# Another written order for the first batch of a fused attention and low-rank mixer kernel

## The chip, the cores and the metric

The kernel runs on one core of a Trainium2 chip. The metric is the device time of one execution in microseconds (us), as the median of several runs. Engines are named as in the profile: PE is TensorE, ACT ScalarE, DVE VectorE, POOL GpSimd, SP the queue that issues most DMAs.

## The reference

Attention with normalised queries and keys, then a mixer and an MLP over its output, for 8 batches, 12 heads, 448 tokens and a head size of 64 (768 = 12 x 64 columns):

```python
q_n, k_n = rmsnorm(q, g_q), rmsnorm(k, g_k)          # x / sqrt(mean(x*x) + 1e-6) * g, over the 64
scores = (q_n @ k_n.T) / sqrt(64)
attn = exp(scores - max); attn = attn / sum(attn)
x = (attn @ v) laid out as [batch, 448, 768]
h = x.transpose(0, 2, 1) @ U @ V                      # mixes the 448 tokens, rank 32
u = x + h.transpose(0, 2, 1)
out = u + relu(u @ w_ch1) @ w_ch2                     # 768 -> 3072 -> 768
```

All inputs and the output are float32; the products run in bf16.

## The kernel before

Heads go in **groups** of four (three groups a batch, numbered through: group 0 to 2 are batch 0), and the attention works on **pairs** of heads, six a batch. Of each group, q and k are loaded by SP, squared (`sq`, line 141 on ScalarE, line 144 on GpSimd), summed over the 64 on VectorE (`sm`, line 167), and turned into roots on ScalarE as a logarithm and an exponential (`rt`, lines 944 and 950 or 953). The rows are then scaled (`sc`, line 957), transposed on TensorE into a PSUM tile (`turn`, line 368) and copied out: q on ScalarE or VectorE with the product of both gains (`tq`, lines 375 and 377), k on VectorE (`tk`, lines 383 and 386). Group 0 is cut in two parts along the tokens (`sqp`, `smp`, `rt0`, `scp`, with the part as their last number: part 0 is 512 elements a partition wide, part 1 is 384), so that its first steps can run on two engines at once.

A pair has four score steps (`S.pair.row`, line 430): rows 0 to 2 are 128 keys for both heads of the pair, row 3 the last 64 keys of both. Each score step writes one of two PSUM tiles of its pool, and an exponential on ScalarE (`E.pair.row`, line 435) empties it; so S.5.1 has to wait for E.4.3. Rows 0 to 2 are 128x896 exponentials, row 3 is 128x448. Then come the products with v (`V.pair.half`, lines 500 and 504) on TensorE and the division by the sum (`N.pair.half`, lines 513 and 514) on VectorE. `val` casts the values of a group on GpSimd (lines 206 and 208), and the loads of the group three further on are issued behind it.

For batch 0 the mixer is done in chunks of columns: `mt` (line 648) multiplies the tokens by U, `mtc` (line 652) copies the result, `mix` (lines 657 to 660) multiplies by V and adds x, `mc` (lines 664 and 666) copies the mixed, transposed columns into `uT`, and `u` (line 711) are the first products with `w_ch1`, for 4 of its 24 slices of 128 columns. `prepu` and `prepv` (lines 342, 343, 333 and 335, GpSimd) lay U and V out for this, and `ms` (`fill_mixer`) fills the buffers with zeros and ones beforehand, among them the margins of a key buffer. `b.n` are n matmuls of 128x128 on the identity (line 245), whose result nobody reads: they only keep TensorE running. Their tile comes from the same pool of four PSUM banks as the transposes and the products. `w` issues a load of a part of `w_ch1` from GpSimd's queue, in the order of the list `todo` (768, 1152, 1152 and 1536 KB); `gr`, `gains`, `pg` and `gg` prepare the product of the gains.

All of batch 0 up to there is a list of steps written out by hand, the string `FRONT`. A step is a name, its numbers, and after a colon its engine (a, v, p for ScalarE, VectorE, GpSimd). The program is recorded in this order, and each engine runs its own instructions in the order of recording, waiting for what they need:

```python
for step in FRONT.split():
    step, _, eng = step.partition(":")
    name, *a = step.split(".")
    steps[name](*map(int, a), engines[eng])
    if name == "val":
        load(int(a[0]) + 3)
```

Behind `FRONT` a planner goes through the attention of the other batches (`att`) and the MLP (`mlp`, from `up`, line 693, on) by costs and due times; it starts from fixed values there, so that what `FRONT` does doesn't change its order. The up-products use slices of `w_ch1` as they come (`up`, line 693), the down-products `w_ch2` (`down`, line 740).

Of the kernel before, what the change touches and what calls it, by code (L numbers as in the profile page):

```python
# [27 lines left out]
def kernel(  # L28
# [13 lines left out]
    nc = tc.nc  # L42
    B, H, S, D = q.shape
# [209 lines left out]
    def fill_values(i, eng):  # L253
        va, vl = va_bufs[i], vl_bufs[i]
        eng.memset(va[:, :, D:D1], 1.0)
        eng.memset(vl, 0.0)
        for e in range(2):
            eng.memset(vl[e * R:(e + 1) * R, :, e * D1 + D:(e + 1) * D1], 1.0)

    def fill_keys(i, eng):  # L260
        eng.memset(kT_bufs[i][D:P, :, SM:S], 0.0)
        eng.memset(kT_bufs[i][0:D, :, S:], 0.0)

    for i in range(2):
        fill_values(i, nc.vector)
    fill_keys(0, nc.vector)
    for e in range(2):
        nc.gpsimd.tensor_mul(gp[:, e * D:(e + 1) * D], grow[:, 0, :], grow[:, 1, :])

    gg = consts.tile([P, 2], FP32)  # L270
# [74 lines left out]
    def fill_mixer():  # L345
        nc.gpsimd.memset(Uz, 0.0)
        fill_values(2, nc.gpsimd)
        fill_keys(1, nc.gpsimd)


    at = {"pe": 0.0, "act": 0.0, "dve": 0.0}
# [429 lines left out]
    for i, (b, pr) in enumerate(pairs):  # L781
        if b == 0:
            continue
        gi, a = divmod(i, 2)
# [85 lines left out]
    for b in range(B):  # L870
# [24 lines left out]
    mlp.extend((3.9 * w, down_end, (B - 1, cols[-1], piece), B - 1) for piece, w in enumerate((1.0, 0.67, 0.34)))  # L895

    FRONT = """
        sqp.0.1:a sqp.0.0:p gr smp.0.1 sqp.1.1:a sqp.1.0:p smp.0.0 rt0.0.1 smp.1.1 gains:p smp.1.0 rt0.1.1 pg rt0.0.0 b.22
        scp.0.1:v scp.1.1:p rt0.1.0 scp.0.0:v sq.1.0:a scp.1.0:p gg turn.0.0 sm.1.0 ms tq.0.0:a turn.0.1 b.17 w tk.0.0 rt.1.0
        sq.1.1:a tq.0.1:v S.0.1 sc.1.0:v S.0.0 b.13 sq.2.0:p E.0.0 sm.1.1 turn.1.0 E.0.1 S.0.2 val.0 tk.0.1 E.0.2 tq.1.0:v b.5  # L900
        sm.2.0 S.0.3 b.8 E.0.3 S.1.0 rt.1.1 tq.1.1:v sq.2.1:p S.1.1 V.0.1 E.1.0 sc.1.1:v b.7 E.1.1 S.1.2 turn.1.1 sm.2.1 E.1.2
        S.1.3 V.0.0 tk.1.0 val.1 E.1.3 N.0.1 rt.2 tk.1.1 sc.2.0:p sc.2.1:v S.2.0 V.1.0 E.2.0 S.2.1 prepu N.1.0 E.2.1 S.2.2
        N.0.0 V.1.1 w E.2.2 turn.2.1 N.1.1 prepv S.2.3 b.4 tk.2.0 E.2.3 S.3.0 E.3.0 tk.2.1 S.3.1 w turn.2.0 V.2.0 E.3.1 tq.2.1:v
        S.3.2 N.2.0 mt.0 E.3.2 tq.2.0:v S.3.3 V.2.1 val.2 mtc.0 E.3.3 S.4.0 N.2.1 E.4.0 S.4.1 V.3.1 w V.3.0 E.4.1 N.3.1 S.4.2
        mix.1 N.3.0 E.4.2 S.4.3 sq.3.0:p mt.1 mc.1:v E.4.3 S.5.0 mtc.1 E.5.0 S.5.1 V.4.0 sq.3.1:p V.4.1 E.5.1 N.4.0 S.5.2 mix.0
        N.4.1 E.5.2 S.5.3 mix.2 mc.0:v mix.3 E.5.3 sm.3.0 u.0.0 mc.2:a u.1.0 mt.2 mc.3:a u.0.1 u.1.1 mtc.2 V.5.0 sm.3.1 u.2.0
        u.2.1 V.5.1 N.5.0 rt.3 u.3.0 u.3.1 N.5.1 u.0.3 u.1.3 u.2.3 u.3.3 mt.3 u.0.2 mix.4 mtc.3 u.1.2 mix.5 mc.4:a u.2.2 u.3.2
        mc.5:a u.0.4 u.1.4 u.2.4 u.3.4 u.0.5 u.1.5 u.2.5 u.3.5
    """
    engines = {"a": nc.scalar, "v": nc.vector, "p": pool, "": None}  # L910
    beside = uT.rearrange("p k c -> p (k c)")[:, :4 * NT * D].bitcast(FP32).rearrange("p (j d) -> p j d", d=D)
# [43 lines left out]
    def scale_by(gi, i, eng, lo=0, hi=NT):  # L955
# [8 lines left out]
        "smp": lambda i, p, eng: sums_part(i, *PARTS[p]),  # L964
        "rt0": lambda i, p, eng: (log_part(i, p), root_part(i, p)),
        "ms": lambda eng: fill_mixer(),
        "scp": lambda i, p, eng: scale_by(0, i, eng, *PARTS[p]),
        "gr": lambda eng: most_gain(),
# [82 lines left out]
    while ia < len(att) or im < len(mlp):  # L1051
# [10 lines left out]
        if take_att:  # L1062
            c, f, a = att[ia]
# [13 lines left out]
        else:  # L1077
# [6 lines left out]
            c, f, a, _ = mlp[im]  # L1084
# [35 lines left out]
```

## Time and profile before

| | us |
|---|---|
| median of 3 runs | 572.04 |
| lowest and highest | 571.39, 573.68 |
| the profiled execution, its own time | 570.46 |
| its span in the profile | 568.7 |
| TensorE busy in the span | 561.5 |
| ScalarE busy in the span | 308.5 |

The granted clock of TensorE is 0.999 of full speed in the profiled execution. In the lines of the profile a time in front of a row is its start in us from the span's start, then its length; `x4` behind it counts instructions that were merged into one row. Brackets show how long the engine was idle before it, and what ended that. Rows of one engine may overlap a little, as an instruction begins before the one ahead has quite ended.

### The profile page before, as it was taken

The numbers are of one execution on the slowest core, as the hardware profiler recorded it, in microseconds if no ns is written. First come the engines' busy times: TensorE is split into PE (matmuls) and PEld (weight loads), VectorE is DVE, ScalarE is ACT, GpSimd is POOL, SyncE is SP. The second block draws the span as 40 slices with busy tenths as digits, with TensorE's granted clock in tenths as the row PEclk, the third lists the DMA queues.
The fourth block names the chain that finished last, engine by engine and source line by source line (L and its number), as shares of the span: only waits on it lengthen the run. The fifth ranks groups of instructions, "written<-read, shape, count | busy, mean of one in ns | idle before, by whom it ended". The sixth has DMA issues, their size and how long they took to land.

```text
span 568.7 us, 11567 instructions
## 1 busy us (share of the span) xinstructions
PE 561.5 (99%) x4756; PEld 321.9 (57%) x4756; DVE 189.4 (33%) x425; ACT 308.5 (54%) x518; POOL 204.5 (36%) x308
## 2 busy tenths in 40 slices
PE   8899999999999999999999999999999999999997
PEld 7665555555555555555556555565465555555555
DVE  6955564312443222521235231532034210410011
ACT  6967760888454776287553677367752544014300
POOL 6874784355332724343522532351531000000000
PEclk9999999999999999999999999999999999999999
DMA  9999999784247633595335735375215200320022
GB/s 241 223 242 240 247 228 179 159 225 114 62 91 171 170 98 63 90 233 144 74 96 107 203 90 125 67 204 128 36 33 86 56 23 0 77 56 0 1 57 56
DMA packets 104830, 68.20 MB, mean 120 GB/s; under 512 B 66633, under 2 KB 100937, under 8 KB 104777
## 3 DMA queue, kind: packets, MB, share of 16 engines
q1 hardware_dynamic: 95124, 57.83, 44.2%
q0 software_dynamic: 9408, 9.44, 10.0%
q8 instruction: 37, 0.61, 0.5%
q10 hardware_dynamic: 244, 0.20, 0.1%
q14 instruction: 17, 0.13, 0.1%
HBM read 52.20 MB, written 11.01 MB: 111 GB/s over the span
## 4 chain that ended last, share of the span: by engine, by line
PE 94%; ACT 4%; DMA 1%; DVE 0%; POOL 0%; issue 0%; POOLq 0%
PE po L740 38%; PE ph L693 37%; PE pv L541 4%; ACT E L435 3%; PE sc L464 2%; PE sl L455 2%; PE sl L476 2%; PE pr L568 1%; PE po L727 1%; PE pv L537 1%; PE sc L430 1%; PE sc L711 1%; PE sc L626 1%; PE pu L609 1%; DMA ob<-in_g_k_dram 1%; PE pt L368 1%
## 5 line engine op out<-in xcount | busy, mean ns | idle before, releaser
L693 PE MATMUL ph<-uT,w1b 128*128 128x448 bf16 x1128 | 223.9, 352 | 0.0
L740 PE MATMUL po<-w2b,hT 128*128 128x384 bf16 x1296 | 223.5, 326 | 0.0
L740 PEld LDWEIGHTS <-hT 128*128 128x128 bf16 x1296 | 122.8, 98 | 84.1 <-issue 7.0
L693 PEld LDWEIGHTS <-w1b 128*128 128x128 bf16 x1128 | 108.2, 98 | 97.6 <-issue 2.2
L700 ACT ACTIVATE hT<-ph 128x448 bf16<-128x448 f32 x187 | 99.7, 550 | 106.9 <-PE ph L693 106.5
L399 POOL TENSOR_SCALAR qT<-qT,gg 128x448 bf16<-128x448 bf16 x36 | 50.4, 1402 | 92.4 <-DMA qT<-qn 77.3
L457 ACT ACTIVATE E<-sl,gg 128x448 bf16<-128x448 f32 x72 | 41.6, 630 | 76.2 <-PE sl L455 75.3
L198 POOL TENSOR_TENSOR qn<-qf,rs 128x384 bf16<-128x384 f32 x36 | 29.9, 830 | 111.9 <-ACT rs L175 106.1
L468 ACT ACTIVATE E<-sc,gg 128x896 bf16<-128x896 f32 x72 | 68.9, 1019 | 0.0
L750 DVE TENSOR_TENSOR ob<-po,x 128x384 f32<-128x384 f32 x46 | 25.6, 557 | 103.7 <-PE po L740 103.0
L167 DVE TENSOR_REDUCE ssq<-sq 128x14 f32<-128x896 f32 x45 | 47.0, 1078 | 23.9 <-ACT sq L141 23.2
L545 DVE RECIPROCAL r<-pv 128x6 f32<-128x6 f32 x42 | 8.2, 195 | 125.4 <-PE pv L541 125.1
L435 ACT ACTIVATE E<-sc,gg 128x896 bf16<-128x896 f32 (+1 forms) x42 | 37.0, 951 | 1.1 <-PE sc L430 0.7
L541 PE MATMUL pv<-va,E 128*128 128x65 bf16 x756 | 35.4, 194 | 0.0
L541 PEld LDWEIGHTS <-E 128*128 128x128 bf16 x756 | 32.4, 98 | 3.2
L198 POOL TENSOR_TENSOR kp<-kf,rs 128x384 bf16<-128x384 f32 x36 | 29.8, 828 | 0.0
L537 PE MATMUL pv<-vl,E 128*128 128x130 bf16 x126 | 27.6, 219 | 0.0
L633 DVE TENSOR_TENSOR x<-sc,x 128x384 bf16<-128x384 f32 x42 | 20.8, 550 | 17.4 <-PE sc L626 17.4
L546 DVE TENSOR_TENSOR x<-pv,r 128x384 bf16<-128x384 f32 x42 | 23.4, 557 | 1.4
L174 ACT ACTIVATE rs<-ssq,eps 128x28 f32<-128x28 f32 x20 | 6.3, 315 | 32.1 <-DVE ssq L167 32.1
L477 ACT ACTIVATE E<-sl,gg 128x448 bf16<-128x448 f32 x36 | 23.3, 646 | 0.0
L206 POOL CAST va<-vf 128x768 bf16<-128x768 f32 x24 | 20.7, 862 | 0.2 <-DMA vf<-in_v_dram 0.2
(130 smaller groups left out, 426.4 us busy)
## 6 DMA issues: line engine op xcount, KB each, us to landing
qf<-in_q_dram SPq DMA_DIRECT2D x23, 448.0 KB, 3.7
kf<-in_k_dram SPq DMA_DIRECT2D x23, 448.0 KB, 4.9
vf<-in_v_dram SPq DMA_DIRECT2D x48, 192.0 KB, 5.5
out_dram<-ob SPq DMA_DIRECT2D x48, 192.0 KB, 2.7
w2b<-in_moe_w_ch_dram POOLq DMA_DIRECT2D x8, 576.0 KB, 15.3
w1b<-in_moe_w_ch_dram POOLq DMA_DIRECT2D x2, 1152.0 KB, 17.6
vf<-in_v_dram SPq DMA_DIRECT2D x48, 32.0 KB, 5.1
w1b<-in_moe_w_ch_dram POOLq DMA_DIRECT2D x1, 1536.0 KB, 28.5
```

The source lines that it names most:

```text
L167: nc.vector.tensor_reduce(ssqs[gi][:, i, :], sqs.pop((gi, i)), AX, ALU.add)
L198: nc.gpsimd.tensor_tensor(main.rearrange("p (t i) d -> p i t d", i=2), src[:, c, :2 * NJ].rearrange("p (i t) d -> p i t d", i=2), rs[:, c, ...
L399: nc.gpsimd.tensor_scalar(qT[:, a], qT[:, a], gg[:, 0:1], None, ALU.mult)
L435: nc.scalar.activation(es[(b, pr)][:, 2 * r:2 * r + n, :], sc[:, :n, :S], AF.Exp, scale=scal, bias=bias)
L457: nc.scalar.activation(E[:, 4 + i, :], ts[i], AF.Exp, scale=scal, bias=bias)
L468: nc.scalar.activation(E[:, 2 * r:2 * r + 2, :], tiles[r][:, :, :S], AF.Exp, scale=scal, bias=bias)
L537: nc.tensor.matmul(pv[:, i].rearrange("p e d -> p (e d)"), E[:, 2 * NJ, w:w + P], vl[:, lp, :], start=True, stop=False)
L541: nc.tensor.matmul(pv[:, i, e, :], E[:, 2 * j + e, w:w + P], va[:, (lp + 2 * e) * NJ + j, :], start=False, stop=(e == 1 and j == NJ - 1))
L693: nc.tensor.matmul(ph, w1b[:, dt, ht * P:(ht + 1) * P], uT[:, dt, off:off + S], start=(dt == 0), stop=(dt == KD - 1))
L700: nc.scalar.activation(hT[:, ht, off:off + S], ph, AF.Relu)
L740: nc.tensor.matmul(po, hT[:, ht, col:col + P], w2b[:, ht, half * HALF:(half + 1) * HALF], start=(ht == 0), stop=(ht == KH - 1))
L750: nc.vector.tensor_tensor(ob[:, h], po, urows(b, col, half), ALU.add)
```

## The change

`FRONT` is written anew: the same steps (other fillers apart) in another order, some on another engine. Two lines around it move the margins of the second key buffer to VectorE, at the kernel's start, from GpSimd within `ms`. What is different in it:

- In group 0, part 0 of k is squared on ScalarE and part 1 on GpSimd, where it was the other way round. Part 1 of q is scaled on GpSimd and part 1 of k on VectorE, also the other way round; part 0 stays (q on VectorE, k on GpSimd). The gains are prepared earlier.
- The q square of group 1 (`sq.1.0`) is on GpSimd, where it was on ScalarE. Its roots (`rt.1.0`) stand behind the first exponential E.0.0, where they stood before it. On ScalarE the order is now q copy, k square, E.0.0, q roots of group 1, E.0.1, E.0.2, k roots, E.0.3.
- The q scale of group 1 (`sc.1.0`) is on GpSimd, where it was on VectorE; the k scale stays on VectorE.
- There are 120 fillers in 9 places instead of 76 in 7; in front of the first transposes 26 instead of 22.
- `ms` stands behind group 2's scale, directly before `prepu`. The second and third `w` stand right behind `val.1`, the fourth behind `val.2`.
- `mix.0` and `mix.1` stand earlier, `mix.3` and `mix.2` change places, the copies `mc.0` and `mc.1` stand before the last norms of pair 4, and the sums of group 3 stand earlier among VectorE's steps.

The whole of it:

```diff
-    fill_keys(0, nc.vector)
+    for i in range(2):
+        fill_keys(i, nc.vector)
...
     def fill_mixer():
         nc.gpsimd.memset(Uz, 0.0)
         fill_values(2, nc.gpsimd)
-        fill_keys(1, nc.gpsimd)
...
     FRONT = """
-        sqp.0.1:a sqp.0.0:p gr smp.0.1 sqp.1.1:a sqp.1.0:p smp.0.0 rt0.0.1 smp.1.1 gains:p smp.1.0 rt0.1.1 pg rt0.0.0 b.22
-        scp.0.1:v scp.1.1:p rt0.1.0 scp.0.0:v sq.1.0:a scp.1.0:p gg turn.0.0 sm.1.0 ms tq.0.0:a turn.0.1 b.17 w tk.0.0 rt.1.0
-        sq.1.1:a tq.0.1:v S.0.1 sc.1.0:v S.0.0 b.13 sq.2.0:p E.0.0 sm.1.1 turn.1.0 E.0.1 S.0.2 val.0 tk.0.1 E.0.2 tq.1.0:v b.5
-        sm.2.0 S.0.3 b.8 E.0.3 S.1.0 rt.1.1 tq.1.1:v sq.2.1:p S.1.1 V.0.1 E.1.0 sc.1.1:v b.7 E.1.1 S.1.2 turn.1.1 sm.2.1 E.1.2
-        S.1.3 V.0.0 tk.1.0 val.1 E.1.3 N.0.1 rt.2 tk.1.1 sc.2.0:p sc.2.1:v S.2.0 V.1.0 E.2.0 S.2.1 prepu N.1.0 E.2.1 S.2.2
-        N.0.0 V.1.1 w E.2.2 turn.2.1 N.1.1 prepv S.2.3 b.4 tk.2.0 E.2.3 S.3.0 E.3.0 tk.2.1 S.3.1 w turn.2.0 V.2.0 E.3.1 tq.2.1:v
-        S.3.2 N.2.0 mt.0 E.3.2 tq.2.0:v S.3.3 V.2.1 val.2 mtc.0 E.3.3 S.4.0 N.2.1 E.4.0 S.4.1 V.3.1 w V.3.0 E.4.1 N.3.1 S.4.2
-        mix.1 N.3.0 E.4.2 S.4.3 sq.3.0:p mt.1 mc.1:v E.4.3 S.5.0 mtc.1 E.5.0 S.5.1 V.4.0 sq.3.1:p V.4.1 E.5.1 N.4.0 S.5.2 mix.0
-        N.4.1 E.5.2 S.5.3 mix.2 mc.0:v mix.3 E.5.3 sm.3.0 u.0.0 mc.2:a u.1.0 mt.2 mc.3:a u.0.1 u.1.1 mtc.2 V.5.0 sm.3.1 u.2.0
-        u.2.1 V.5.1 N.5.0 rt.3 u.3.0 u.3.1 N.5.1 u.0.3 u.1.3 u.2.3 u.3.3 mt.3 u.0.2 mix.4 mtc.3 u.1.2 mix.5 mc.4:a u.2.2 u.3.2
-        mc.5:a u.0.4 u.1.4 u.2.4 u.3.4 u.0.5 u.1.5 u.2.5 u.3.5
+        sqp.0.1:a sqp.0.0:p gr smp.0.1 gains:p sqp.1.0:a smp.0.0 sqp.1.1:p pg b.26 rt0.0.1 smp.1.0 rt0.0.0 scp.0.1:p smp.1.1
+        rt0.1.0 scp.0.0:v rt0.1.1 scp.1.0:p scp.1.1:v turn.0.0 sq.1.0:p gg turn.0.1 tq.0.0:a b.14 tk.0.0 sq.1.1:a S.0.0 w sm.1.0
+        S.0.1 b.17 E.0.0 sm.1.1 sq.2.0:p rt.1.0 S.0.2 b.18 E.0.1 tk.0.1 E.0.2 tq.0.1:v S.0.3 val.0 b.8 sm.2.0 rt.1.1 S.1.0 b.10
+        E.0.3 sc.1.1:v sc.1.0:p E.1.0 S.1.1 V.0.1 E.1.1 turn.1.1 S.1.2 sq.2.1:p tk.1.0 turn.1.0 E.1.2 S.1.3 V.0.0 tq.1.0:v E.1.3
+        tq.1.1:v S.2.0 N.0.1 E.2.0 val.1 S.2.1 b.11 sm.2.1 E.2.1 S.2.2 V.1.0 N.0.0 rt.2 tk.1.1 w V.1.1 E.2.2 S.2.3 sc.2.1:v b.9
+        w E.2.3 S.3.0 N.1.1 turn.2.1 E.3.0 sc.2.0:p N.1.0 S.3.1 V.2.1 E.3.1 tk.2.0 S.3.2 b.7 tk.2.1 E.3.2 ms turn.2.0 S.3.3
+        prepu V.2.0 tq.2.0:v E.3.3 tq.2.1:v S.4.0 prepv N.2.0 mt.0 E.4.0 S.4.1 mtc.0 V.3.0 val.2 E.4.1 S.4.2 N.3.0 V.3.1 E.4.2
+        N.2.1 w S.4.3 mix.0 N.3.1 E.4.3 mix.1 S.5.0 mc.0:v S.5.1 E.5.0 V.4.1 mc.1:v sq.3.0:p mt.1 N.4.1 E.5.1 S.5.2 V.4.0 mtc.1
+        E.5.2 sm.3.0 mix.3 sq.3.1:p mix.2 S.5.3 u.0.0 N.4.0 E.5.3 u.1.0 u.0.1 u.1.1 mc.2:a mt.2 sm.3.1 u.2.0 V.5.0 V.5.1 mtc.2
+        rt.3 N.5.0 mix.4 mc.3:a u.2.1 N.5.1 u.3.0 mc.4:a u.3.1 u.0.3 u.1.3 mt.3 u.2.3 u.3.3 mtc.3 u.0.2 u.1.2 u.2.2 mix.5 u.3.2
+        u.0.4 mc.5:a u.1.4 u.2.4 u.3.4 u.0.5 u.1.5 u.2.5 u.3.5
     """
```

## The prediction

> **What bounds the kernel now.** I read the page first, for the engine that is never idle.
>
> ```profile
> span 568.7 us, 11567 instructions
> PE 561.5 (99%) x4756; PEld 321.9 (57%) x4756; DVE 189.4 (33%) x425; ACT 308.5 (54%) x518; POOL 204.5 (36%) x308
> ...
> PE 94%; ACT 4%; DMA 1%; DVE 0%; POOL 0%; issue 0%; POOLq 0%
> ```
>
> TensorE is busy for 99% of the span and makes 94% of the chain that ended last. ScalarE has 4% of it, and the change touches only the first batch, so the next question is where those 4% lie. The chain of waits in order of time, then the table of busy time by stretch:
>
> ```profile
> 26.27 3.34 ACT E L435 x4
> 29.61 0.04 issue
> 29.66 0.35 PE sc L430
> ```
>
> ```profile
> 9.50:29.66 20.16, 18.45 (x259) 12.88 (x260) 18.47 (x50) 19.38 (x31) 17.68 (x30) 1.00 1.09 227
> 29.66:39.46 9.80, 9.80 (x118) 6.60 (x118) 6.51 (x14) 5.97 (x11) 6.93 (x7) 1.00 1.13 245
> ```
>
> After the time and length of a stretch these rows give the busy time of PE, PEld, DVE, ACT and POOL, then the granted clock, the DMA share and GB/s. From 9.50 to 29.66 ScalarE works 19.38 of 20.16 us: the first batch's exponentials are the bound. From 29.66 TensorE has no gap up to 39.46, where the up-products of the main loop begin. So 29.66 is the turning point. It is the score step S.5.1, and it waits for the end of exponential E.4.3 (29.61), whose PSUM tile it takes. What the change is worth is how far this point moves, plus what it shifts in TensorE's own queue behind it. All instructions after the written order stand in the same order in both kernels.
>
> **The change, part by part.** Times here are those of the profiled execution: span 568.7, its own time 570.46 us; the three timed runs have a median of 572.04, so I carry the difference over to that. ScalarE's timeline:
>
> ```profile
> 7.31 0.30 ACT L937 ACTIVATE rs<-ssq,eps 128x6 f32<-128x6 f32 x1 [0.83 <-DVE ssq L157]
> ...
> 8.63 0.93 ACT L141 ACTIVATE sq<-qf 128x896 f32<-128x896 f32 x1
> 10.10 0.63 ACT L375 ACTIVATE qT<-pt,gg 128x448 bf16<-128x448 bf16 x1 [0.55 <-PE pt L368]
> 10.71 0.31 ACT L944 ACTIVATE rs<-ssq,eps 128x14 f32<-128x14 f32 x1
> 11.05 0.19 ACT L953 ACTIVATE rp<-rs 128x14 f32<-128x14 f32 x1
> 11.17 0.93 ACT L141 ACTIVATE sq<-kf 128x896 f32<-128x896 f32 x1
> 12.01 3.31 ACT L435 ACTIVATE E<-sc,gg 128x896 bf16<-128x896 f32 x4
> 15.20 0.32 ACT L944 ACTIVATE rs<-ssq,eps 128x14 f32<-128x14 f32 x1
> ...
> 15.66 3.31 ACT L435 ACTIVATE E<-sc,gg 128x896 bf16<-128x896 f32 x4
> 18.85 0.33 ACT L944 ACTIVATE rs<-ssq,eps 128x28 f32<-128x28 f32 x1
> ...
> 19.43 13.55 ACT L435 ACTIVATE E<-sc,gg 128x896 bf16<-128x896 f32 x16
> ```
>
> *First exponential.* Before, it starts at 12.01, at once behind the k square of group 1 (11.17, 0.84 to the next start), which stands behind the pair of group 1's q roots (10.71 to 11.17, 0.46) and the copy of q (10.10). The change takes the roots out of this place. The q square (8.63) goes to GpSimd; where it stood, ScalarE then idled 0.55, so its leaving gives nothing by itself. The copy waits for the transposes of q, these for the scaled q and k:
>
> ```profile
> 5.07 1.03 POOL L154 TENSOR_TENSOR sq<-qf 128x512 f32<-128x512 f32 x1
> 6.07 1.03 POOL L154 TENSOR_TENSOR sq<-kf 128x512 f32<-128x512 f32 x1
> 7.19 0.18 POOL L280 TENSOR_SCALAR ob<-ob 1x1 f32<-1x1 f32 x1
> 7.45 0.18 POOL L281 TENSOR_SCALAR ob<-ob 1x1 f32<-1x1 f32 x1
> 7.93 1.91 POOL L957 TENSOR_TENSOR kp<-rs,kf 128x384 bf16<-128x384 f32 x2 [0.30 <-ACT rs L940]
> 9.79 0.52 POOL L346 MEMSET x<- 128x512 bf16 x1
> ...
> 11.24 1.07 POOL L295 DMA_DIRECT2D w1b<-in_moe_w_ch_dram  x1
> 12.33 1.71 POOL L144 TENSOR_TENSOR uT<-qf 128x896 f32<-128x896 f32 x1
> ...
> 33.72 1.08 DVE L167 TENSOR_REDUCE ssq<-sq 128x14 f32<-128x896 f32 x1
> ```
>
> ```profile
> 9.90 0.55 PE L368 MATMUL pt<-ident,kp 128*128 128x128 bf16 x7
> 10.29 1.11 PE L245 MATMUL busy<-ident 128*128 128x128 bf16 x17
> 11.34 0.36 PE L430 MATMUL sc<-qT,kT 64*128 64x448 bf16 x2
> ```
>
> GpSimd's new queue: q square to 6.07, the two gain steps to 6.6 (0.27 each, start to start), the 384-wide k square to about 7.4 (0.77 if it goes with width, 1.03 at most), then the two scales, 1.91 together: k complete at 9.3 instead of 9.84. Its k root is ready by then, as ScalarE has only the four small root pairs in line (three stand between 7.31 and 8.63, 0.44 each). The q scale on VectorE ends earlier than before too. So q and k are transposed by about 9.85 (before: 9.90 + 0.55), and the k copy on VectorE starts near 10.0. Before, S.0 started only at 11.34, when 17 fillers from 10.29 were through, (1.11 - 0.22)/16 = 0.056 us each; now 14 stand there, and S.0.0 comes near 10.7. ScalarE copies q from about 9.35, squares k of group 1 and is free at 10.8. The first exponential then starts near 10.7 + 0.36 = 11.06: **0.95 earlier**. If only k's gain counts, 0.55.
>
> *Roots behind the exponentials.* Group 1's q roots now stand behind E.0.0, and 0.46 goes back: **+0.46**. Their sum must be there by 11.95 (11.06 + 0.89): GpSimd's new square runs 9.3 to 10.95 (1.71, row at 12.33), and the sum takes VectorE 1.0 more (1.08, the last row there, whose end overlaps the next start). That just fits; if it slips, ScalarE waits that long. The other roots only change places.
>
> [...]
>
> *Fillers.* Behind the first transposes 94 fillers instead of 54, or 40 x 0.056 = 2.2 us more of TensorE. In the stretch to 29.66 TensorE was idle 20.16 - 18.45 = 1.71, and fillers were 54 x 0.056 = 3.0; now 5.3 must fit into 4.7, an overrun of 0.55 by that count. The count is pessimistic, because a matmul's row holds its whole 355 ns though the next follows sooner:
>
> ```profile
> L430 PE MATMUL sc<-qT,kT 64*128 64x448 bf16 (+1 forms) x38 | 7.7, 355 | 0.9 <-ACT E L435 0.6
> ```
>
> Ends are 0 and 2.2; I take **+0.1**, nearest to the waits on exponentials that this row names, which fillers merely occupy.
>
> *GpSimd's later queue.* The fills of the mixer (9.79 to 11.24 before; the key fills among them go to VectorE's idle start) move behind group 2's scale, and two load issues (about 0.9 each) stand ahead, so U is prepared some 2.5 later. Cover: its reader mt.0 stands behind S.4.0. If mt.0 waits, S.4.1 is queued behind it, with about 0.7 us (an exponential's 0.89 less the score's own time) before E.4.1 wants it. I take 0; the loss would be the excess over 0.7.
>
> *TensorE behind the turning point.* mix.0 and mt.1 change sides of S.5.1, the chunk copies change engines' order; worth -0.2 to +0.3. I take 0.
>
> *Weight loads.* The first moves from 11.24 to about 10.6. The second and third now stand right behind the casts of group 1's values, ahead of group 2's scale:
>
> ```profile
> 20.01 0.29 POOL L208 CAST vl<-vf 64x128 bf16<-64x128 f32 x1 [0.73 <-DMA vf<-in_v_dram]
> ...
> POOL vl L208 <- DMA vf<-in_v_dram: 1.6, 2, 0.8
> ...
> 22.55 0.90 POOL L295 DMA_DIRECT2D w1b<-in_moe_w_ch_dram  x1
> ```
>
> (The line without a time is from the list of waits.) Up to these casts GpSimd has the new square and group 1's q scale (1.7 each, at the width of the row at 12.33) instead of the fills (1.45): 1.9 more, against 1.6 that it waited there for landings. So they end near 20.3 in either kernel, and the second load starts then instead of at 22.55, while the loads of group 3 are on their way. The price is rival A's; of its likely 0 to 1.1 us I take **+0.1**.
>
> Sum: -0.95 + 0.46 + 0.1 + 0.1 = **-0.3 us**: 570.2 in a profiled execution, **571.7** against the median of 572.04. A measurement of this kernel can tell about 0.5%, 2.9 us, from no change: this is no change.
>
> **Rivals.** *A, the loads collide (slower).* Group 3's k load and group 4's, from the list of DMA issues:
>
> ```profile
> kf<-in_k_dram SPq DMA_DIRECT2D x1, 448.0 KB, 7.1
> ...
> kf<-in_k_dram SPq DMA_DIRECT2D x1, 448.0 KB, 15.2
> ```
>
> ```profile
> 21.89 0.41 SPq L101 DMA_DIRECT2D kf<-in_k_dram  x1
> ...
> 26.78 0.60 SPq L101 DMA_DIRECT2D kf<-in_k_dram  x1
> ...
> 29.43 1.67 POOL L144 TENSOR_TENSOR sq<-kf 128x896 f32<-128x896 f32 x1
> ```
>
> Issued before the second weight load was under way, k took 7.1 us; issued after, 15.2. The k sum of group 3 also moves up on VectorE, from 33.72 to about 32.5 (chunk copies that stood ahead of it come earlier), with a copy that the mixing products wait for now queued behind it. The square must thus begin by 30.85, and k (landed at 21.89 + 7.1 = 29.0) may come 1.85 late for nothing; each us beyond costs one. If it fares like group 4's, it lands at 37.1 and the price is 8.1 - 1.85 = 6.2: 577.9. With the weight load 2.3 earlier I expect one to three us of delay, a price of 0 to 1.1. It decides from 1.85 us on, and exceeds 0.5% from about 5.
>
> [...]
>
> *B, fillers on the path.* If TensorE becomes the bound before the turning point, the 2.2 us come on top: 571.7 + 2.1 = 573.8. Against it: ScalarE is 96% busy there. For it: the overrun of 0.55.
>
> *C, the lead carries through.* If the exponentials run with fewer gaps (16 take 13.5 from 19.43; at the pace of the first four, 12.01 to 15.20, they would take 12.8, and 0.6 of the difference lies before the turning point), it comes 0.95 - 0.46 + 0.6 = 1.1 earlier: 570.9.
>
> **How the numbers follow.** Forecast (571.0 to 572.6) 0.70; A 0.13, half of it beyond 0.5%; B 0.11, C 0.06. Both signs' small cases lie within 0.5%. The three runs before spread from 0.65 below their median to 1.64 above. The range goes from C less 0.6, 570.3, to B plus 0.6, 574.4; beyond it lies the far part of A. Faster by over 0.5% (below 569.2) 0.03; slower (above 574.9) 0.08; the same 0.89.
>
> **What would show it.** Right: the first exponential near 11.06, S.5.1 between 29.1 and 29.5, TensorE without a gap behind it, up-products from 39.0 to 39.5. Wrong: VectorE idle before a group-3 sum with a DMA or GpSimd named (A); fillers running to the start of a score with ScalarE idle (B); ScalarE waiting for a root's sum behind E.0.0; or a difference that arises after 40 us, where I expect none.

## The result, and the profile after

The changed kernel takes 574.88 us (median of 15 runs, 572.50 to 579.99) against 572.52 (15 runs, 570.98 to 574.98): a ratio of **1.0056, 95% interval 1.0031 to 1.0081**. It is slower, by a little more than the 0.5% I had named as the limit of what can be told from no change; 574.88 is 0.5 us above my range, and I had forecast -0.3 us where +2.4 came. The profiled execution takes 578.58 us (span 576.8) and is one of the longer ones, so its profile shows more loss than the median has.

The page of the changed kernel: busy time by engine, and the chain that ended last.

```profile
span 576.8 us, 11655 instructions
PE 566.5 (98%) x4800; PEld 325.4 (56%) x4800; DVE 189.0 (33%) x426; ACT 308.5 (53%) x517; POOL 206.9 (36%) x308
...
PE 92%; DMA 4%; ACT 2%; DVE 1%; SPq 0%; POOL 0%; issue 0%; POOLq 0%; ACTq 0%
```

ScalarE's 4% of the chain have become 2%, and DMA has gone from 1% to 4%. Its place is seen in the chain in order of time (start, length, what) and in the first up-product on TensorE's timeline, which came at 39.46 before:

```profile
24.50 12.87 DMA kf<-in_k_dram
...
37.51 1.69 POOL sq L144
...
39.22 1.09 DVE ssq L167
40.31 0.21 DVE x L652
...
40.56 0.55 PE ph L657
```

```profile
47.59 1.30 PE L693 MATMUL ph<-uT,w1b 128*128 128x448 bf16 x6
```

The chain runs through the load of group 3's k. GpSimd squares it (`sq`), VectorE sums it (`ssq`), and only then VectorE copies a chunk of the mixing (L652) that TensorE waits for. From the first up-product to the end both executions take the same: 576.8 - 47.59 = 529.2 and 568.7 - 39.46 = 529.2. The whole difference of 8.1 us between these two executions arises ahead of it. Busy time by stretch (length, then PE, PEld, DVE, ACT, POOL, granted clock, DMA share, GB/s):

```profile
9.50:29.66 20.16, 18.20 (x270) 13.30 (x267) 15.41 (x42) 17.99 (x27) 16.59 (x24) 1.00 0.98 181
29.66:39.46 9.80, 7.50 (x111) 5.36 (x110) 5.21 (x14) 5.40 (x8) 5.12 (x7) 0.96 1.13 251
39.46:47.59 8.13, 7.05 (x35) 3.63 (x34) 3.46 (x8) 2.21 (x6) 4.48 (x6) 0.63 1.13 234
```

TensorE is idle for 1.96 + 2.30 + 1.08 = 5.3 us in these rows, against 1.71 before up to its first up-product. And its clock is halved for a time: 0.04 x 9.80 + 0.37 x 8.13 = 3.4 us of full-speed work are missing, as much as 6.8 us at half speed take away. The two together, 3.6 more of idling and up to 3.4, are most of the 8.1; what is left is within the 2.2 us that the 40 more fillers were estimated at, which count as busy. This is an account of one execution, not a test of each part. The waits on the timelines of GpSimd, SyncE, VectorE and TensorE:

```profile
22.61 1.72 POOL L296 DMA_DIRECT2D w1b<-in_moe_w_ch_dram  x2
...
34.26 1.67 POOL L144 TENSOR_TENSOR sq<-qf 128x896 f32<-128x896 f32 x1 [2.03 <-DMA qf<-in_q_dram]
37.51 1.68 POOL L144 TENSOR_TENSOR sq<-kf 128x896 f32<-128x896 f32 x1 [1.58 <-DMA kf<-in_k_dram]
```

```profile
24.50 0.41 SPq L101 DMA_DIRECT2D kf<-in_k_dram  x1
```

```profile
35.97 1.09 DVE L167 TENSOR_REDUCE ssq<-sq 128x14 f32<-128x896 f32 x1 [2.69 <-POOL sq L144]
39.22 1.09 DVE L167 TENSOR_REDUCE ssq<-sq 128x14 f32<-128x896 f32 x1 [1.62 <-POOL sq L144]
```

```profile
37.65 0.38 PE L648 MATMUL pu<-x 128*128 128x128 bf16 x4 [2.30 <-DVE x L514]
40.56 0.55 PE L657 MATMUL ph<-Vr,x 128*128 128x448 bf16 x1 [1.08 <-DVE x L652]
```

The second and third weight loads are issued on GpSimd from 22.61, and SyncE issues group 3's k only at 24.50. Before, k went first (21.89) and the second load followed (22.55). Now k takes 12.9 us instead of 7.1. Group 3's q, issued one place ahead of k (23.87), is late as well: its square starts at 34.26, after a wait of 2.03 for the landing, where it started at 27.78 before. VectorE stands 2.69 us before the sum of q and 1.62 before the sum of k, and TensorE waits 2.30 and 1.08 for what is queued behind them. So the larger wait hangs on q; where "late k" is written below, both loads are meant, which stand next to each other in SyncE's queue.

### The profile page after: what moved, and what is told of

Its sections match the earlier page's. It is cut to its first block, busy times and chain, and to the rows that moved or that the text cites. A ratio compares the mean times of both kernels' runs of the same rounds, so it can differ in the third digit from the quotient of the medians.

```text
span 576.8 us, 11655 instructions
## 1 busy us (share of the span) xinstructions
PE 566.5 (98%) x4800; PEld 325.4 (56%) x4800; DVE 189.0 (33%) x426; ACT 308.5 (53%) x517; POOL 206.9 (36%) x308
## 4 chain that ended last, share of the span: by engine, by line
PE 92%; DMA 4%; ACT 2%; DVE 1%; SPq 0%; POOL 0%; issue 0%; POOLq 0%; ACTq 0%
PE po L740 37%; PE ph L693 37%; PE pv L541 4%; DMA kf<-in_k_dram 4%; PE sc L464 2%; PE sl L455 2%; ACT E L435 2%; PE sl L476 2%; PE pr L568 1%; PE po L727 1%; PE pv L537 1%; PE sc L711 1%; PE sc L626 1%; PE sc L430 1%; PE pu L609 1%; PE pt L368 0%
## 5 line engine op out<-in xcount | busy, mean ns | idle before, releaser
L435 ACT ACTIVATE E<-sc,gg 128x896 bf16<-128x896 f32 (+1 forms) x42 | 37.4, 951 | 2.4 <-PE sc L430 2.1
## 6 DMA issues: line engine op xcount, KB each, us to landing
w2b<-in_moe_w_ch_dram POOLq DMA_DIRECT2D x8, 576.0 KB, 12.1
```

The costliest lines, as they stand in the source:

```text
L435: nc.scalar.activation(es[(b, pr)][:, 2 * r:2 * r + n, :], sc[:, :n, :S], AF.Exp, scale=scal, bias=bias)
```

## The experiments

Two theories stood after the two profiles. *The order of the loads* (rival A): k is late because the weight loads are under way when it is issued. *SyncE's queue* ("theory 1" in the expectations): the first weight load, now 0.6 earlier, holds up group 1's values, SyncE's issues behind these slip, and k is issued 2.6 us later. Each ratio below is against the kernel before on the same chip.

**Both kernels again.**

> The changed kernel unaltered, for a second profile of it: the first shows group 1's k landing at 11.23 (9.78 before) and group 3's k at 37.4 (28.98 before). Theory 1 (the loads of SyncE's queue are held up, first of all by the first weight load): time 574 to 576, group 3's k again lands later than 33. Theory 2 (that late landing was an accident of one execution): k of group 3 lands by 31 and the first up-product comes before 41.

> The kernel before unaltered, for a second profile of it. If the late landing of group 1's q and k in the changed kernel's profiles (q 7.8 to 9.6, k 10.1 to 11.8 in five of them) comes from the changed order: here q lands near 7.1 and k near 9.8 again. If it varies from execution to execution: anywhere from 7 to 9.6 and 9.7 to 11.8, and SyncE's later issues shift with it.

The changed kernel: 576.17, ratio 1.0045 (1.0021 to 1.0069), k issued at 24.38 and taking 12.6 us. So the late k is no accident. The kernel before, one run: 573.94, and its profile upset my reading of the first one. The list of waits, SyncE's and GpSimd's timelines, the list of DMA issues (its last column is the time from issue to landing), and the first up-product:

```profile
SPq L321 <- DMA vf<-in_v_dram: 2.4, 1, 2.4
```

```profile
25.06 0.41 SPq L101 DMA_DIRECT2D kf<-in_k_dram  x1
```

```profile
23.12 1.69 POOL L957 TENSOR_TENSOR qn<-rs,qf 128x896 bf16<-128x896 f32 x1
24.75 0.32 POOL L342 CAST Ub<-x 128x160 bf16<-128x160 f32 x1
25.01 0.29 POOL L343 CAST x<-x 128x128 bf16<-128x128 f32 x1
25.25 0.90 POOL L295 DMA_DIRECT2D w1b<-in_moe_w_ch_dram  x1
```

```profile
kf<-in_k_dram SPq DMA_DIRECT2D x1, 448.0 KB, 8.4
```

```profile
42.12 1.30 PE L693 MATMUL ph<-uT,w1b 128*128 128x448 bf16 x6
```

Here the *unchanged* order has SyncE waiting 2.4 us for group 1's values before it can issue V (first line, from the list of waits), and k is issued at 25.06, later than in the changed kernel. Theory 1 falls as an effect of the change: that slip comes and goes by execution (the runs were on several chips, so it may also go by chip). What stays is the order. Between the casts of group 1's values and the second weight load GpSimd still has group 2's scale (1.69) and the casts of U, and these 2.1 us keep the load just behind k's issue, 0.2 us here and 0.7 in the first profile. k then takes 8.4 us, and no sum waits. The change takes just these two steps out from in front of the load. The first up-product at 42.12 instead of 39.46 also shows that my first profile was an early one.

**The second and third load later, in the changed kernel.**

```
-... tk.1.1 w V.1.1 E.2.2 S.2.3 sc.2.1:v b.9 w E.2.3 ... prepu V.2.0 ... prepv N.2.0
+... tk.1.1 V.1.1 E.2.2 S.2.3 sc.2.1:v b.9 E.2.3 ... prepu w V.2.0 ... prepv w N.2.0
```

> The changed kernel with the second and third weight loads moved back behind the casts of U and V on GpSimd, as before (issued near 28 instead of 22.61 and 23.5). Rival A of the prediction (these loads share the DMA engines with group 3's k): k takes 7 to 9 us from its issue instead of 12.87, lands near 32, the wait before the group 3 sums shrinks from 4.3 us in all to 1 or less, time 571.5 to 573. Theory 1 (the delay comes from the first load and SyncE's queue): k is still issued at 24.5, gains at most 2 us, time 574 to 575.

574.75, ratio 1.0012 (0.9989 to 1.0035). k is issued no earlier to speak of (23.79), but ahead of the loads (25.61). It takes 8.7 us, the sums start without a wait, the clock stays whole, and the first up-product comes 7.0 us earlier than in the changed kernel's profile (the span is only 5.3 us shorter, as 530.9 us follow instead of 529.2; where that goes was not traced):

```profile
25.61 0.90 POOL L296 DMA_DIRECT2D w1b<-in_moe_w_ch_dram  x1
```

```profile
kf<-in_k_dram SPq DMA_DIRECT2D x1, 448.0 KB, 8.7
```

```profile
32.72 1.09 DVE L167 TENSOR_REDUCE ssq<-sq 128x14 f32<-128x896 f32 x1
34.36 1.09 DVE L167 TENSOR_REDUCE ssq<-sq 128x14 f32<-128x896 f32 x1
```

```profile
40.59 1.30 PE L693 MATMUL ph<-uT,w1b 128*128 128x448 bf16 x6
```

**The same loads earlier, in the kernel before.**

```
-... val.1 E.1.3 ... V.1.1 w E.2.2 ... S.3.1 w turn.2.0
+... val.1 w w E.1.3 ... V.1.1 E.2.2 ... S.3.1 turn.2.0
```

> The kernel before with its second and third weight loads moved right behind the casts of group 1's values, as the changed kernel has them. Rival A as the prediction described it: the loads are issued near 20.3 and 21.2 ahead of group 3's k (issue near 21.9), whose landing moves from 28.98 to 33 to 35; the group 3 sums on VectorE come 2 to 4 us later, but stand behind more of the mixing's copies than in the changed kernel: ratio 1.000 to 1.004. Theory 1 (SyncE's issues also have to slip for the full loss): the k load is not issued later than before, its landing moves by less than 3 us, ratio 1.000.

575.50, ratio 1.0032 (1.0008 to 1.0055). This one edit makes the kernel before slower and gives it the same picture: loads at 22.05, k at 24.00, taking 13.5 us, waits before both sums, the first up-product at 46.45.

```profile
22.05 1.72 POOL L295 DMA_DIRECT2D w1b<-in_moe_w_ch_dram  x2
```

```profile
kf<-in_k_dram SPq DMA_DIRECT2D x1, 448.0 KB, 13.5
```

```profile
36.23 1.08 DVE L167 TENSOR_REDUCE ssq<-sq 128x14 f32<-128x896 f32 x1 [1.40 <-POOL sq L144]
39.39 1.09 DVE L167 TENSOR_REDUCE ssq<-sq 128x14 f32<-128x896 f32 x1 [1.87 <-POOL sq L144]
```

**One load alone.** The third `w` of the changed kernel goes behind `prepu`, the second stays.

> The changed kernel with its third weight load alone moved behind the cast of U; the second stays ahead of group 2's scale (issue near 22). If one load ahead is enough to keep group 3's k waiting: k takes 11 us or more from its issue, ratio 1.003 to 1.006. If both loads are needed: k takes 9 to 11 us and lands near 34, ratio 1.001 to 1.003.

578.31, ratio 1.0071 (1.0046 to 1.0097). The second load (23.23, ahead of k at 25.13) is enough: k takes 12.9 us, and the sums wait 3.02 and 1.56. This also speaks against another cause, that the issues keep GpSimd from other work. In the kernel before with the loads early TensorE waits 1.09 us for group 2's scale, which stands behind both issues on GpSimd. Here one issue stands ahead of it, there is no such wait, and the loss is not smaller.

All profiles in which k keeps its place in SyncE's queue fall into two groups:

| kernel | second load | k issued | k takes | first up-product | ratio |
|---|---|---|---|---|---|
| changed | 22.61 | 24.50 | 12.9 | 47.59 | 1.0056 |
| changed, again | 22.47 | 24.38 | 12.6 | 45.25 | 1.0045 |
| third load later | 23.23 | 25.13 | 12.9 | 48.53 | 1.0071 |
| 80 fillers (below) | 21.54 | 23.24 | 11.7 | 44.29 | 1.0054 |
| first load later (below) | 21.32 | 23.86 | 11.4 | 43.06 | 1.0012 |
| sums later (below) | 22.41 | 24.52 | 12.1 | 40.96 | 0.9994 |
| before, loads early | 22.05 | 24.00 | 13.5 | 46.45 | 1.0032 |
| before | 22.55 | 21.89 | 7.1 | 39.46 | 1 |
| before, again | 25.25 | 25.06 | 8.4 | 42.12 | |
| second and third load later | 25.61 | 23.79 | 8.7 | 40.59 | 1.0012 |

With the second load ahead k takes 11.4 to 13.5 us; with k ahead, 7.1 to 8.7 (4.7 to 9.9 in the five further profiles, whose first up-products come at 40.10 to 44.49). Each row is one profiled execution, and the ratio is of all runs, so the two need not follow each other row by row. With the second load ahead and the sums left in place the ratios are 1.0032 to 1.0071, but for 1.0012 with the first load later; with k ahead, 1.0006 to 1.0022.

**The sums of group 3 later on VectorE.** The loads stay; the sums go behind the mixing's copies, the roots behind ScalarE's last chunk copy.

```
-... sm.3.0 mix.3 ... mt.2 sm.3.1 u.2.0 ... rt.3 N.5.0 ... mtc.3 u.0.2 ... mc.5:a u.1.4
+... mix.3 ... mt.2 u.2.0 ... N.5.0 ... mtc.3 sm.3.0 sm.3.1 u.0.2 ... mc.5:a rt.3 u.1.4
```

> The changed kernel with both sums of group 3 moved on VectorE behind all of the mixing's copies (and the roots of group 3 behind ScalarE's last chunk copy); nothing changes in the loads. If a late k costs time only because the in-order VectorE stands before its sum: k lands as late as in the changed kernel, no wait of TensorE on VectorE around 35 to 41, the first up-product near 39.5, time 571.5 to 573. If the time is lost elsewhere (fillers, the mixing's order): 574.9, as the changed kernel.

573.91, ratio 0.9994 (0.9974 to 1.0014). k takes 12.1 us as in the changed kernel, and it costs little: the first up-product comes at 40.96. So a late k is paid for because the in-order VectorE stands before the sums with the mixing's copies behind them. At 56.41 TensorE then waits 1.36 us before a score, where the kernel before has no such wait; whether that is the late k's doing was not tried.

**Group 3's q and k ahead of U, V and group 2's values on SyncE.** A step of its own issues the five kinds of loads in this order right behind the scaling of group 0; weight loads, fillers and sums stay as the change has them. The second kernel is the kernel before with the same edit.

> The changed kernel with the loads of group 3's q and k issued ahead of those of U, V and group 2's values on SyncE; weight loads, fillers and sums stay as the change has them. If a late k is the whole loss: k lands before 28 whatever the weight loads do, VectorE does not wait before the group 3 sums, ratio 0.998 to 1.001. If the weight loads then delay the next ones in the queue by as much (U and V, for the mixing; group 2's values): U or V lands late, the mixing waits, ratio 1.003 to 1.006.

> The kernel before with the same loads early. Its k did not make VectorE wait in either profile (28.98 and 33.42), so if only that wait counts: ratio 1.000. If U and V, pushed back by two loads of 448 KB, become late for the mixing: 1.002 to 1.005.

Changed: 577.82 (6 runs), ratio 1.0068 (1.0047 to 1.0088). k is there in time, and now the next ones in line are late: group 2's values. GpSimd's and TensorE's timelines:

```profile
32.13 0.83 POOL L206 CAST va<-vf 128x768 bf16<-128x768 f32 x1 [2.16 <-DMA vf<-in_v_dram]
```

```profile
35.01 0.27 PE L500 MATMUL pv<-vl,E 128*128 128x130 bf16 x1 [2.76 <-POOL vl L208]
```

Before: 573.31, ratio 0.9994 (0.9971 to 1.0018). My theory that a late k is the whole loss falls in this form. In the changed kernel the first of group 2's four value loads is issued at 22.99 and the second weight load at 23.21, ahead of the other three. In the kernel before the second weight load comes at 25.85, behind all four (from 23.14), and it does not mind the other order on SyncE. So the weight loads in front most likely delay what follows them on SyncE, whatever that is. At 26.73 TensorE also waits 1.64 us for group 2's scale, which GpSimd has behind the issues; this run does not part the two.

**Fillers (rival B).** The changed kernel with 54 fillers behind the first transposes instead of 94, alone and together with the later loads.

```
-... S.0.1 b.17 E.0.0 ... S.0.2 b.18 E.0.1 ... b.8 ... b.10 ... b.11 ... b.9 ... b.7
+... S.0.1 b.9 E.0.0 ... S.0.2 b.9 E.0.1 ... b.5 ... b.5 ... b.6 ... b.3 ... b.3
```

> The changed kernel with 80 fillers instead of 120, 54 of them behind the first transposes as before. Rival B (fillers on the path): 40 x 0.056 = 2.2 us come back, ratio 1.0010 instead of 1.0045 to 1.0056. If the wait for group 3's k decides (theory 1), whatever TensorE gains ahead of it is lost in that wait: ratio 1.0045 to 1.0056 as the changed kernel, with VectorE still idle before both group 3 sums. If fewer fillers let the clock fall, slower still.

> The changed kernel with the second and third weight loads behind the casts of U and V (ratio 1.0012 with 120 fillers) and with 80 fillers. With those loads later TensorE was busy for 20.15 of the 20.50 us from 9.5 to 30. If fillers are then on the path: up to 2.2 us less, ratio 0.998 to 1.000. If they only fill waits: 1.001, TensorE with more idle time from 9.5 to 30 and the first up-product at the same place, 40 to 41.

Alone: 575.91, 1.0054 (1.0028 to 1.0080), no change. With the later loads: 573.71, 1.0006 (0.9988 to 1.0024), against 1.0012 with all fillers. Up to 2.2 us (0.4%) were to be had; the medians show 0.06%. Rival B finds no support, though intervals this wide don't exclude a part of the 0.4%.

**The first exponential ahead of k's square.** `sq.1.1:a` goes behind `E.0.0`, with the later loads, with 80 and with 120 fillers.

> As the kernel with later weight loads and 80 fillers, and ScalarE's square of group 1's k moved behind the first exponential. If the first exponential waits for nothing but that square, that is for group 1's k to land (10.1 to 11.8 in the profiles), it now starts near 10.9 whenever k lands, 0.5 to 1.8 us earlier, and the ratio is 0.996 to 0.999. If the lead is lost again behind it (the roots, group 2's late k), the ratio equals that of the kernel without the move.

> The same move of the square with all 120 fillers. If fillers bound TensorE from 9.5 to 30, an earlier first exponential brings nothing here: ratio 1.001 as without it, first up-product 40.5. If they do not: 0.997 to 0.999, as with 80 fillers.

573.80, 1.0015 (0.9999 to 1.0031), and 573.40, 1.0011 (0.9991 to 1.0031): no gain over 1.0006 and 1.0012, though the first exponential starts at 10.97 and 11.14, where I had predicted it. ScalarE's timeline with 120 fillers shows where the lead goes:

```profile
11.14 1.01 ACT L435 ACTIVATE E<-sc,gg 128x896 bf16<-128x896 f32 x1 [0.95 <-PE sc L430]
12.04 0.94 ACT L141 ACTIVATE sq<-kf 128x896 f32<-128x896 f32 x1
...
13.33 1.89 ACT L435 ACTIVATE E<-sc,gg 128x896 bf16<-128x896 f32 x2
```

ScalarE now idles 0.95 before the exponential instead of before the square, and the second exponential starts at 13.33, against 13.42 and 13.69 without the move. The square and the roots stand ahead of it in either case.

**The first weight load.** Later in the changed kernel (behind `sq.2.0:p`, ahead of `val.0`), and earlier in the kernel before (ahead of `ms`).

> The changed kernel with the first weight load moved behind group 2's q square on GpSimd (issued near 14.8 instead of 10.64). Theory 1: group 1's values land before 18, the load of V is issued near 17.5 instead of 20.15, group 3's k by 22.5 instead of 24.50 and lands by 34; time 572 to 573.5. Rival (the second and third weight loads alone make k late): k of group 3 still lands after 36, time 574.9 as the changed kernel.

> The kernel before with the first weight load ahead of the mixer's fills on GpSimd (issued near 9.8 instead of 11.24). Theory 1: group 1's first value load lands at 19 to 20 (16.42 before), the load of V, which stands eight loads behind it in SyncE's queue, is issued only then, and group 3's k is issued near 24.5 instead of 21.89, behind the second weight load; it lands at 35 to 37 as in the changed kernel. Time 1.002 to 1.006 of before. Rival (the first load is harmless, only the second and third matter): k issued by 22.5, ratio 1.000.

574.58, 1.0012 (0.9992 to 1.0031), and 575.03, 1.0022 (1.0001 to 1.0043). In the first, V is issued at 17.73, but U then lands later (SyncE waits 1.5 us for it) and k is still issued at 23.86, behind the second load. It takes 11.4 us and lands at 35.3, about 2 us earlier than in the changed kernel, and the sums wait 0.95 and 1.68: in the profile, less of the same loss. In the second, k is issued at 25.53 ahead of the second load (25.90) and takes 8.4 us; no sum waits. Its profile is late from the start, with group 1's q landing 2.5 us later than in the first profile of before and the first up-product at 44.49, so whether the earlier first load costs something by itself stays open. The interval only just leaves 1.

**Everything together.** The first, second and third load later and the sums later; and early q and k with the second and third load later and 80 fillers.

> The changed kernel with the three edits together: first weight load behind group 2's q square, second and third behind the casts of U and V, the group 3 sums behind the mixing's copies. If the three work on one chain (a late k before an in-order VectorE), they do not add up: whichever takes the wait away takes it all, and the ratio is 0.997 to 1.000, as with the sums alone (0.9994). If each has a loss of its own, it comes to 0.9994 less 0.003 for each of the loads, 0.993 to 0.995. The first up-product comes near 39.5.

> The changed kernel with group 3's q and k early, the second and third weight loads behind the casts of U and V, and 80 fillers: all the losses named so far are taken away, so what is left is the gain of the order itself. By the prediction's sum, -0.3 us: ratio 0.9995. If the roots behind the exponentials and the rest bring more: 0.996 to 0.998. If group 1's late k takes the gain: 1.000 to 1.002.

573.36, 1.0010 (0.9989 to 1.0030), and 573.49, 1.0000 (0.9986 to 1.0015). The edits do not add up; each takes away the one wait. And with the wait gone the new order is worth nothing that can be measured. No version is measurably faster than the kernel before: no interval lies below 1.

## Why the prediction was wrong

**The step that failed is *Weight loads*, with its price in rival A.** I wrote that the second load would start near 20.3 instead of 22.55, "while the loads of group 3 are on their way", and expected k to be one to three us late, a price of 0 to 1.1. The rows quoted beside it said otherwise: k issued before the second load took 7.1 us, issued after it 15.2. With the load at 20.3 and k at 21.89 by my own count, k was issued *after*, and I should have taken the second row. I interpolated between two cases where there is a switch, and gave 0.13 to what was the likely one. What the runs showed in its place: k issued behind the load took 11.4 to 13.5 us in seven profiles, and moving the second and third load alone, in either kernel, switches k between the two times. My sum had +0.1 us for it; by the ratios with and without these loads in front, measured side by side (1.0045 and 1.0012, whose intervals overlap), it is about 1.9. Rival A was right in what it said would come: "if it fares like group 4's, it lands at 37.1", price 6.2, 577.9. It landed at 24.50 + 12.9 = 37.4. That the two landings agree is luck: k was issued 2.6 us later than in the count and took 2.3 less than group 4's. (The load started at 22.61, not 20.3, and k's issue slipped to 24.50. The order was as computed.) Its price of 6.2 stands between the 8.1 of the two profiles and the 2.4 of the medians: 577.9 is close to the 578.58 of one long execution, but above the interval of the ratio (574.3 to 577.2 us). Executions differ in how much of the wait shows.

**The slack was worked out for k alone.** k's square had to begin by 30.85. It began at 37.51, so by that count 6.7 us were to be lost, and 8.1 came, but not by that sum. The larger wait hangs on q, whose slack I never worked out. S.5.1, which I had put at 29.1 to 29.5, came at 31.3 (its row, shared with S.5.0, starts at 31.11), 1.7 later than before and ahead of either wait. And the halved clock, up to 3.4, was not in the prediction. That the sums stand ahead of the mixing's copies on VectorE is the other half of the cause: with the sums behind these, a k as late costs nothing measurable. That the change moved them up is not needed for it, as the kernel before, where they stand further back, loses 1.0032 with the loads early.

***First exponential*, -0.95: did not come.** It starts at 12.17 instead of 11.06, behind the square of group 1's k, which waits for its load. ScalarE's timeline of the changed kernel:

```profile
9.60 0.63 ACT L375 ACTIVATE qT<-pt,gg 128x448 bf16<-128x448 bf16 x1 [1.15 <-PE pt L368]
11.31 0.95 ACT L141 ACTIVATE sq<-kf 128x896 f32<-128x896 f32 x1 [1.08 <-DMA kf<-in_k_dram]
12.17 0.99 ACT L435 ACTIVATE E<-sc,gg 128x896 bf16<-128x896 f32 x1
```

In the other profiles of this order of steps it starts anywhere from 11.33 to 13.20, and with the old order from 12.01 to 13.20. The copy of q came at 9.60, near the 9.35 predicted. But I never asked when the operand of the next step lands: in the profile of before k was there for its square at 11.17, and no row showed a wait. Where the exponential was let off first, the lead was worth nothing.

**What was taken as the bound.** "ScalarE works 19.38 of 20.16 us" was true of one execution. In the second profile of the kernel before, with the same instructions, it works 17.76 of 20.50 from 9.50 on as group 2's k and group 1's values land later. Which of the two bounds the front, landings or exponentials, changes between executions: S.5.1 comes at 29.7 in the first profile of before and at 32.3 in the second, a difference far above the 0.3 us that I had forecast.

***GpSimd's later queue*, 0: right for U only.** mt.0 does not wait for U. But the two load issues also stand ahead of group 2's scale, which the sum didn't have. TensorE waits for it, and ScalarE behind TensorE:

```profile
26.14 0.56 PE L368 MATMUL pt<-ident,qn 128*128 128x128 bf16 x7 [0.51 <-POOL qn L957]
```

```profile
26.93 0.63 ACT L435 ACTIVATE E<-sc,gg 128x448 bf16<-128x448 f32 x1 [0.64 <-PE sc L430]
```

In the changed kernel's second profile this wait is not there, so it is not what the medians turn on; its price was not measured by itself.

**Right:** *fillers* cost nothing that can be measured (1.0054 against 1.0056), and behind the first up-product both executions take 529.2 us. My sum without the weight loads, -0.4 us or 0.9993, lies within the intervals of the kernels that have their loads behind (1.0000, 1.0006, 1.0012). That proves little: its largest term, the first exponential, did not come, and these intervals hold 1 as well. *Roots behind the exponentials* was not measured by itself.

## What to carry to other kernels

Ask of a load that is moved not how much earlier it starts but which loads it passes: here a 448 KB load took 5 to 10 us ahead of the weights and 11 to 14 behind them, and the margin that kept the order was 0.2 to 0.7 us of GpSimd's work. A step taken out from in front of such an issue removes a tie that no wait in the profile shows. Work out the slack of every load that is passed, not of the last one alone: here q, one place ahead of k, made the larger wait. And take a second profile of the unchanged kernel before sizing slacks of one or two us: group 3's k landed at 29.0 in one and at 33.5 in the other.

## What the runs showed of the hardware

**Landings differ between executions.** SyncE's first load of group 2's k waits until group 1's q has landed, 1.6 us in the changed kernel's profile. In the first profile of the kernel before it was issued at 7.22, in its second at 8.81, in the others between 7.39 and 10.25, with the same issues ahead of it. The runs were on several chips, so executions and chips are not told apart here.

**SyncE's issues waited for landings of other tiles.** V's load waits 2.0 us in the changed kernel for group 1's values, which go into another tile. This wait, those of group 2's two k loads (1.6 and 1.7 us) and that of one of U's (0.5) all name the load eight places ahead in SyncE's order. In the trace that load reports its landing to the same semaphore as the one that waits (number 108 for V): from SyncE's seventh load to V's, eight numbers go round, 101 to 105 and 107 to 109. Whether anything but these semaphores sets the eight is not shown. In these four places the queue stood for the 0.5 to 2.0 us.

**TensorE's clock stood at half after short stalls.** Stretches of 3.41 us of four kernels, columns as above:

```profile
35.31:38.72 3.41, 1.11 (x25) 0.98 (x24) 1.60 (x3) 0.35 (x1) 1.83 (x2) 1.00 1.14 235
38.72:42.14 3.42, 2.34 (x22) 1.51 (x20) 2.31 (x6) 1.50 (x4) 3.26 (x4) 0.50 1.16 226
42.14:45.55 3.41, 3.41 (x14) 1.60 (x13) 1.39 (x2) 0.00 (x0) 1.80 (x4) 0.50 1.11 225
45.55:48.96 3.41, 3.41 (x23) 1.88 (x22) 0.00 (x0) 2.08 (x3) 0.16 (x1) 1.00 1.11 259
```

```profile
24.74:28.16 3.42, 1.78 (x31) 1.31 (x28) 1.09 (x5) 1.65 (x3) 3.20 (x9) 1.00 0.94 171
28.16:31.57 3.41, 3.27 (x48) 2.20 (x47) 2.44 (x9) 3.19 (x4) 1.31 (x3) 1.00 1.14 223
31.57:34.98 3.41, 0.68 (x9) 0.35 (x6) 1.18 (x3) 2.12 (x3) 1.41 (x3) 1.00 1.15 209
34.98:38.40 3.42, 3.39 (x35) 2.40 (x35) 1.66 (x4) 0.97 (x1) 3.21 (x3) 0.50 1.15 230
```

```profile
11.07:14.49 3.42, 1.64 (x22) 1.23 (x21) 1.94 (x2) 2.72 (x5) 2.19 (x3) 1.00 0.92 151
14.49:17.90 3.41, 2.91 (x20) 1.52 (x20) 3.24 (x7) 3.35 (x7) 3.27 (x5) 0.50 1.09 215
```

```profile
18.79:22.20 3.41, 1.78 (x31) 1.05 (x28) 3.30 (x10) 2.57 (x7) 0.21 (x1) 1.00 1.11 293
22.20:25.62 3.42, 3.42 (x33) 2.37 (x32) 3.28 (x13) 2.75 (x4) 3.10 (x6) 0.50 0.57 161
```

The first fence is the changed kernel, the second the one with q and k early, the third the one with the square behind the exponential and 80 fillers, the fourth the kernel before with q and k early. After a stretch with TensorE busy for 0.68, 1.11 or 1.64 us the clock is at half; at 1.78 it went both ways, to full in the second fence and to half in the fourth. In the second kernel the clock stood at half from 34.98 to 38.40, one such stretch, and in the changed kernel from 38.72 to 45.55, two of them. A stretch need not be idle for it: one busy for 1.64 of 3.42 us was followed by half the clock (third fence). A half-rate stretch busy for 2.34 was followed by a second one (first fence). In the changed kernel's profile that is how 3.6 us of waiting became up to 7. But the halved clock is not what sets the medians apart. The kernel before has such a stretch too, in its second profile from 22.00 to 25.41. In the second run of the changed kernel the executions at a granted clock of 0.999 and above have a median of 575.44 (7 of 12), and those of the kernel before beside it 573.19 (16 of 35): without halved stretches the difference is 2.3 us, near the 2.6 of all.
